# Expert weight preparation in halves over nine attention turns, and bulk transfers behind a slot's transposes, in an attention and two-layer mixture-of-experts kernel

## The chip, the cores and the metric

The kernel runs on one core of a Trainium2 chip. The metric is the device time of one execution in microseconds, the median of several runs; lower is better.

## What is computed

Attention with pooled keys, then two mixture-of-experts layers that send each token to one of eight experts:

```python
kv_pool = kv.reshape(B, H // r, r, W // r, r, C).mean(axis=(2, 4))
k = v = kv_pool.reshape(B, -1, C) @ w_sr
s = scale * (q @ k.transpose(0, 2, 1))
a = np.exp(s - s.max(-1, keepdims=True))
a /= a.sum(-1, keepdims=True) + 1e-09
x = (a @ v).reshape(B * S, D)
...
expert_idx = np.argmax(logits, axis=1)
for e in range(E):
    mask = expert_idx == e
    h = np.maximum(x[mask] @ w1[e], 0.0)
    out[mask] = gate_w[mask, None] * (h @ w2[e])
```

B is 2, there are 24,576 queries in all, 768 keys a batch, C and D are 128, E is 8 and the hidden size F is 1024. The first layer takes its logits from `x @ w_gate`, the second from the normalized rows and expert embeddings over `tau`.

## The kernel before

**Attention** works on 48 groups of 512 tokens. `plan` is a list of steps, each with a lag in turns: in turn n the step `K3:3` is done for group n - 3, tile 3. A turn therefore holds steps of seven groups, and every engine takes its instructions in this written order (`ordered` ties them). Per tile of 128 tokens: scores on TensorE (`at_K`, L531), negated row maxima on VectorE (`at_N`, L538), exponentials on ScalarE (`at_E`, L545), then two 16-bit parts whose sum is the probability, the high part on ScalarE (`at_S`, L552) or VectorE (`at_D`), the low part on VectorE (`at_Z`, L561). SP issues a DMA that transposes both parts (`at_t`, L568) into one of three buffers `aT`; the products with the values read them (`at_A`, L575 to L577), ScalarE copies the sum to `xT` (L582), TensorE multiplies by the first layer's gate (`at_R`, L603), and the routing (`route`) ends with four indirect DMAs of GpSimd that put the rows to their experts' places in DRAM (L491). While the first batch runs, the second batch's `kv` is loaded in pieces of 512 KB (L187).

**Weight preparation.** Matmuls in 16 bits need each weight as a high and a low part at a scale of the expert. For one expert this is: load of `w1` and `w2` into `wraw` (`pw_load`, L340 and L341), sum of squares of both (`pw_square`, L350, ScalarE), scales (`pw_dve`), high parts on ScalarE (L358), low parts on VectorE (L374), and the store of `whl` and the scales to DRAM (`pw_store`, L383 and L385). `wraw` and `whl` have one buffer each. It has five phases. In attention, phase p of expert i stands in turn 2 + 9i + 2p: the steps `ul`, `ua`, `ug` and `uw` of `plan` stand for load, ScalarE, VectorE, and store and first square. So five of the first layer's eight experts are ready when attention ends. The other three, and then the scales of the second layer's eight (whose parts are made in the slots), are prepared beside the slots of the first layer by the steps `vl`, `va`, `vg`, `vs` of `plan_1`, five turns an expert, later three.

**Slots.** Both layers work on slots: 512 rows of one expert (`slot_new`). A slot's turn has eight slices; `both` has the steps of both layers, `plan_1` those of the first. `W0` and `W1` load its two weights into one of two buffers if the expert has changed (`slot_w`, L868), `X` loads its rows transposed (`slot_load`, L930), `H` and `Y` are the two products in eight chunks each (L955 to L957, L974 to L976), `h` and `g` the two parts of the ReLU on ScalarE (L960) and VectorE (L965), and `p` and `n` take steps of `slot_post`. In the first layer `slot_post` issues two DMA transposes of the result (L1000), GpSimd adds their two parts (L1012), ScalarE squares them (L1017), and routing for the second layer follows. `H0` is in slice 2 two turns after the slot's number, `Y0` in slice 6 of that turn, the transposes are in slice 7 of the next.

A list of slots is made by `table`, which runs a few small VectorE instructions at each `.` of a plan; there are eight in a slot's turn. At its end it writes 512 rows of zeros behind each expert's rows (L799), 260 KB each.

The first slots begin before attention has ended. The rest of the attention turns is emitted between the slot's steps:

```python
            while pos < (n0 + i + m / len(plan_l) + DN) * len(plan):
                pos = next(rest_, 1 << 30)
```

Here i is the slot's turn and `pos` the place in the attention's steps; `DN` is 0.

Of the kernel before, what the change touches and what calls it, by code (L numbers as in the profile page):

```python
# [8 lines left out]
F32 = mybir.dt.float32  # L9
# [11 lines left out]
P = 128  # L21
C = 128
# [49 lines left out]
def _body(ctx, tc, q, kv, w_sr, w_gate, w1a, w2a, emb, tau, w1b, w2b, out):  # L72
# [261 lines left out]

    def pw_load(i, ph):

        if ph == 0:
            l, e = divmod(i, E)
            raw = p1.tile([P, 2, F], F32, tag="wraw", name=f"wraw{i}")
            SP.dma_start(raw[:, 0, :], (w1a, w1b)[l][e])  # L340
            SP.dma_start(raw[:, 1, :].rearrange("p (f d) -> p f d", d=C),  # L341
                         (w2a, w2b)[l][e].rearrange("(f p) d -> p f d", p=P))
            pw[i] = [raw, None, None, None]

# [6 lines left out]

    def pw_act(i, ph):
        raw, ss, sc, hl = pw[i]
        if ph == 1:
            pw_square(i, 1)
        elif ph in (3, 4) and i < E:
            k = ph - 3
            A.activation(hl[:, 2 * F * k:2 * F * k + F], raw[:, k, :], AF.Copy, scale=sc[:, k:k + 1])  # L358
# [18 lines left out]
    def pw_store(i, ph):  # L377
        if ph == 0:
            pw_square(i, 0)
        if ph == NPH - 1:  # L380
            l, e = divmod(i, E)
            _, _, sc, hl = pw.pop(i)
            ins = [SP.dma_start(WS[l][e * P:(e + 1) * P, :], sc).ins]  # L383
            if l == 0:
                ins.append(SP.dma_start(WT[e * P:(e + 1) * P, :], hl).ins)  # L385
                if e >= EA:
                    for w in ins:
                        for r in w_reads:
                            tc.declare_no_dep(w, r, reason="weights of other experts")
                    w_late.extend(ins)  # L390
# [244 lines left out]
    U0 = 2  # L635
    UW = 2 if NA1 else 1
    UP = 2 * NPH - 1 if NA1 else NPH

    def at_u(g, fn):

        i, ph = divmod(g - U0, UP)
        if 0 <= i < EA and ph % UW == 0 and ph // UW < NPH:
            fn(i, ph // UW)


    def table(info, l, kind, ns, nh=0, prev=None, left=None):
# [149 lines left out]
        if kind != "a":  # L796
            for e in range(E):
                r = sp_val(bi[0:1, e:e + 1], NROW - TG)
                ins = SP.dma_start(XS[l].rows[bass.ds(r, TG), :].rearrange("(p r) c -> p r c", r=4), zrows)  # L799
                XS[l].wrote(ins.ins)  # L800
                if e % 2:
                    yield
            info["upto"] = XS[l].mark()
# [334 lines left out]
    for n, ((i, w0, m), t) in enumerate(zip(parts, tl)):  # L1138
# [13 lines left out]
        if n == 6:  # L1152
# [8 lines left out]
             "Z": at_Z, "t": at_t, "A": at_A, "x": at_x, "r": at_r, "R": at_R, "w": at_w, "l": at_l, "o": at_o, "p": at_p,  # L1161
             "ul": lambda g: at_u(g, pw_load), "ua": lambda g: at_u(g, pw_act),
             "ug": lambda g: at_u(g, pw_dve), "uw": lambda g: at_u(g, pw_store)}
    plan = """
# [53 lines left out]
    def pw_all(steps_):  # L1218
        for i in steps_:
            for fn in (pw_load, pw_act, pw_dve, pw_store):  # L1220
                fn(*divmod(i, NPH))
# [48 lines left out]
    def run(*a):  # L1270
        for _ in turns(*a):
# [4 lines left out]
              "g": slot_hL, "Y": slot_y, "B": slot_raw, "C": slot_hi, "D": slot_lo}  # L1276
    wsteps = {"vl": pw_load, "va": pw_act, "vg": pw_dve, "vs": pw_store}

# [3 lines left out]
    plan_1 = """  # L1282
        - - p:5 p:4 n:5 - p:4 p:4 / W0:1 n:4 p:5 p:4 n:5 - p:5 p:4 p:5 p:4 / X:1 vl:0 p:5 n:5 - p:5 n:4 vg:1 n:4 p:4 /
        - n:4 p:5 n:4 - p:4 p:4 p:4 / - n:4 p:5 - p:4 - vs:1 / p:3 W1:1 n:4 p:5 - - n:4 /
        - p:3 p:3 n:4 p:3 - n:4 va:0 n:4 / - n:4 p:3 - n:4 p:4 - n:4"""
    plan_2 = """
# [29 lines left out]
    last_a = NG + max(lags)  # L1316
    DN = 0

# [93 lines left out]
```

## Time and profile before

| | |
|---|---|
| median of 3 runs | 1737.48 us (1734.93 to 1743.86) |
| profiled execution | 1748.93 us, of which the span of instructions is 1747.2 us |
| mean granted TensorE clock | 0.975 |
| TensorE busy | 1594.9 us, 91% |
| VectorE busy | 1441.0 us, 82% |
| ScalarE busy | 1328.0 us, 76% |
| moved by DMA | 240.61 MB, 138 GB/s on average |

The busy share is an average over attention (up to about 640 us), the first layer (to about 1220 us) and the second. A turn of attention is counted here from one write of `xT` to the next (ScalarE, L582, one for each group), a slot from its first matmul (L955) to that of the next slot. In a view of windows the columns of an engine give its busy time in the window and, in brackets, its instructions; then come the granted clock, the mean busy share of the DMA engines (packets overlap, so that it can pass 1) and the bytes moved per time. In a timeline a bracket at the end of a row gives how long the engine sat idle before it and what ended that.

### The profile page before, as it was taken

How to read it: one execution, taken by the hardware profiler on the slowest of the kernel's cores; microseconds unless marked ns; L12 is line 12 of the kernel's file. 1: busy time of each engine (PE TensorE's matmuls, PEld its weight loads, DVE VectorE, ACT ScalarE, POOL GpSimd, SP SyncE). 2: the span in 40 equal slices, each digit the busy share in tenths (PEclk: the TensorE clock that was granted, in tenths of full speed). 3: DMA queues.
4: the chain of work that ended last, by engine and by line, in shares of the span. 5: the costliest groups of instructions: out<-in, count | busy, mean ns of one | idle time of the engine just before them, and what ended most of it. 6: DMA issues, size and time to landing. Idle time of an engine off the chain costs nothing.

```text
span 1747.2 us, 31671 instructions
## 1 busy us (share of the span) xinstructions
PE 1594.9 (91%) x8713; PEld 890.4 (51%) x8713; DVE 1441.0 (82%) x3887; ACT 1328.0 (76%) x2731; POOL 982.0 (56%) x1298
## 2 busy tenths in 40 slices
PE   6888988989888789899999999998999999999996
PEld 6666656656666534444444444444444444444443
DVE  5898989989899757787788787787998888888875
ACT  3777778878777746776777877776888888888885
POOL 1386665665565646565666666665544444444453
PEclk9899999999999999999999999999999999999998
DMA  7999998999999953444665455445337335343353
GB/s 247 218 236 201 173 225 174 207 209 179 218 181 190 189 108 78 110 109 113 145 160 123 98 112 106 74 95 128 76 77 175 78 76 127 75 83 74 77 121 63
DMA packets 631019, 240.61 MB, mean 138 GB/s; under 512 B 578464, under 2 KB 604202, under 8 KB 629168
## 3 DMA queue, kind: packets, MB, share of 16 engines
q1 hardware_dynamic: 611776, 200.31, 57.5%
q0 software_dynamic: 18752, 38.18, 8.2%
q8 instruction: 70, 1.15, 0.3%
q14 instruction: 117, 0.96, 0.2%
q10 hardware_dynamic: 304, 0.01, 0.0%
HBM read 148.53 MB, written 52.02 MB: 115 GB/s over the span
## 4 chain that ended last, share of the span: by engine, by line
PE 57%; DVE 18%; issue 8%; DMA 7%; ACT 6%; POOL 3%; SPq 0%; POOLq 0%; ACTq 0%; DVEq 0%
PE ps L957 7%; PE ps L955 7%; PE ps L974 7%; PE ps L956 7%; PE ps L976 7%; PE ps L975 7%; PE ps L531 5%; DVE hL L965 4%; DMA aT<-ab 3%; DVE ab L561 3%; DMA rowss<-yHLs 2%; DVE nm L538 2%; PE ps L575 2%; ACT ab L552 2%; PE ps L577 2%
## 5 line engine op out<-in xcount | busy, mean ns | idle before, releaser
L965 DVE SCALAR_TENSOR_TENSOR hL<-ps,hH 128x512 f16<-128x512 f32 (+1 forms) x808 | 540.0, 672 | 168.6 <-ACT hH L960 114.6
L960 ACT ACTIVATE hH<-ps 128x512 f16<-128x512 f32 (+1 forms) x808 | 466.7, 584 | 174.4 <-PE ps L957 144.2
L1075 POOL DMA_INDIRECT out_dram<-rowss,idxs x198 | 211.4, 1068 | 258.9 <-DVE idxs L1072 157.7
L974 PE MATMUL ps<-hH,wbuf 128*128 128x512 f16 (+1 forms) x808 | 304.1, 376 | 7.3 <-ACT hH L960 7.1
L491 POOL DMA_INDIRECT xs<-rowsa,idxa x192 | 202.6, 1055 | 189.5 <-DVE sca L431 143.1
L976 PE MATMUL ps<-hL,wbuf 128*128 128x512 f16 (+1 forms) x808 | 303.9, 376 | 1.3
L975 PE MATMUL ps<-hH,wbuf 128*128 128x512 f16 (+1 forms) x808 | 304.0, 376 | 0.0
L957 PE MATMUL ps<-x,wbuf 128*128 128x512 f16 (+1 forms) x808 | 304.0, 376 | 0.0
L955 PE MATMUL ps<-x,wbuf 128*128 128x512 f16 (+1 forms) x808 | 304.0, 376 | 0.0
L956 PE MATMUL ps<-x,wbuf 128*128 128x512 f16 (+1 forms) x808 | 303.8, 376 | 0.0
L491 POOL DMA_INDIRECT xs<-rowss,idxs x196 | 204.9, 1046 | 61.6 <-issue 26.8
L545 ACT ACTIVATE a<-ps,nm 128x768 f32<-128x768 f32 x192 | 171.9, 896 | 64.2 <-DVE nm L538 63.1
L561 DVE SCALAR_TENSOR_TENSOR ab<-a,ab 128x768 f16<-128x768 f32 x192 | 201.1, 1047 | 9.9 <-ACT ab L552 9.9
L538 DVE TENSOR_REDUCE nm<-ps 128x1 f32<-128x768 f32 x192 | 181.4, 945 | 32.6 <-PE ps L531 17.9
L552 ACT ACTIVATE ab<-a 128x768 f16<-128x768 f32 x192 | 161.1, 839 | 32.2 <-DMA aT<-ab 28.0
L918 DVE SCALAR_TENSOR_TENSOR wbuf<-wbuf,wsl 128x512 f16<-128x512 f32 x204 | 151.9, 745 | 0.0
L575 PE MATMUL ps<-aT,v 128*128 128x512 f16 x288 | 112.9, 392 | 42.8 <-DMA aT<-ab 33.2
L910 ACT ACTIVATE wbuf<-wbuf,wsl 128x512 f16<-128x512 f32 x204 | 146.0, 716 | 4.7 <-DMA wbuf<-in_moe_w_dram 4.6
L531 PE MATMUL ps<-kH,qH 128*128 128x384 f32 x384 | 129.4, 419 | 9.9 <-ACT a L545 8.8
L975 PEld LDWEIGHTS <-wbuf 128*128 128x128 f16 x808 | 79.4, 98 | 94.5 <-issue 11.3
L976 PEld LDWEIGHTS <-wbuf 128*128 128x128 f16 x808 | 79.4, 98 | 92.6 <-issue 2.2
L957 PEld LDWEIGHTS <-wbuf 128*128 128x128 f16 x808 | 79.4, 98 | 92.5 <-issue 2.2
(391 smaller groups left out, 2892.9 us busy)
## 6 DMA issues: line engine op xcount, KB each, us to landing
wbuf<-in_moe_w_dram SPq DMA_DIRECT2D x102, 512.0 KB
wbuf<-wt SPq DMA_DIRECT2D x98, 512.0 KB
wraw<-in_moe_w_dram SPq DMA_DIRECT2D x32, 512.0 KB
q<-in_q_dram SPq DMA_DIRECT2D x48, 256.0 KB
wt<-whl SPq DMA_DIRECT2D x8, 1024.0 KB
kv<-in_kv_dram SPq DMA_DIRECT2D x12, 512.0 KB
xs<-zrows SPq DMA_DIRECT2D x18, 260.0 KB
out_dram<-rowss,idxs POOLq DMA_INDIRECT x198
```

Of the source, the lines that this page charges most:

```text
L491: ins = G.indirect_dma_start(out=XS[l].rows, out_offset=bass.IndirectOffsetOnAxis(ap=idx[:, r:r + 1], axis=0), in_=rows[:, r, 0:RW], in_of ...
L531: PE.matmul(sv[:, h, :], lhsT=d[x][:, P * t:P * (t + 1)], rhs=k[:, 384 * h:384 * (h + 1)], start=k is kH and x == "qH", stop=x == "qL")
L538: V.tensor_reduce(d["nm"][:, t:t + 1], scores(g, t), axis=AX.XY, op=ALU.max, negate=True)
L561: V.scalar_tensor_tensor(ab[:, 1, :], st[g].pop(("a", t)), AS, ab[:, 0, :], op0=ALU.mult, op1=ALU.subtract)
L955: PE.matmul(hb, lhsT=wL, rhs=s.xH, start=True, stop=False)
L956: PE.matmul(hb, lhsT=wH, rhs=s.xH, start=False, stop=False)
L957: PE.matmul(hb, lhsT=wH, rhs=s.xL, start=False, stop=True)
L960: A.activation(hH, ps[:, f % 4, 0:s.W], AF.Relu)
L965: V.scalar_tensor_tensor(hL, ps[:, f % 4, 0:s.W], 0.0, s.h[f][0], op0=ALU.max, op1=ALU.subtract)
L974: PE.matmul(s.acc, lhsT=wL, rhs=hH, start=f == 0, stop=False)
L975: PE.matmul(s.acc, lhsT=wH, rhs=hH, start=False, stop=False)
L976: PE.matmul(s.acc, lhsT=wH, rhs=hL, start=False, stop=f == NF - 1)
```

## The change

- The five experts of attention: load of `w1` in turn 0 of nine and of `w2` in turn 1, the first square in turn 2, the second and the sum over partitions in turn 3, scales in turn 4, the first weight's parts in turn 5 and its store in turn 6, the second's in turns 7 and 8. `pw_store` is split: its store is now `pw_out`.
- In the first layer's slots, `vl` (load), the new `vt` (store) and `W1` (second weight of a slot) move to slice 8, behind the transposes of slice 7.
- `table` pauses twice after each block of zeros; before, once after each second block.
- `DN` is 1: attention's last turns run one turn earlier against the slots.

```diff
-    def pw_load(i, ph):
+    def pw_load(i, ph, parts=(0, 1)):
         if ph == 0:
             l, e = divmod(i, E)
-            raw = p1.tile([P, 2, F], F32, tag="wraw", name=f"wraw{i}")
-            SP.dma_start(raw[:, 0, :], (w1a, w1b)[l][e])
-            SP.dma_start(raw[:, 1, :].rearrange("p (f d) -> p f d", d=C),
-                         (w2a, w2b)[l][e].rearrange("(f p) d -> p f d", p=P))
-            pw[i] = [raw, None, None, None]
+            if 0 in parts:
+                raw = p1.tile([P, 2, F], F32, tag="wraw", name=f"wraw{i}")
+                pw[i] = [raw, None, None, None]
+                SP.dma_start(raw[:, 0, :], (w1a, w1b)[l][e])
+            if 1 in parts:
+                SP.dma_start(pw[i][0][:, 1, :].rearrange("p (f d) -> p f d", d=C),
+                             (w2a, w2b)[l][e].rearrange("(f p) d -> p f d", p=P))
...
+    def pw_out(i, ph, parts=(0, 1)):
         if ph == NPH - 1:
             l, e = divmod(i, E)
-            _, _, sc, hl = pw.pop(i)
-            ins = [SP.dma_start(WS[l][e * P:(e + 1) * P, :], sc).ins]
+            _, _, sc, hl = pw[i]
+            ins = []
+            if 1 in parts:
+                pw.pop(i)
+                ins.append(SP.dma_start(WS[l][e * P:(e + 1) * P, :], sc).ins)
             if l == 0:
-                ins.append(SP.dma_start(WT[e * P:(e + 1) * P, :], hl).ins)
+                c0, c1 = 2 * F * parts[0], 2 * F * (parts[-1] + 1)
+                ins.append(SP.dma_start(WT[e * P:(e + 1) * P, c0:c1], hl[:, c0:c1]).ins)
...
+    turns_u = {("l", 0): lambda i: pw_load(i, 0, (0,)), ("l", 1): lambda i: pw_load(i, 0, (1,)),
+               ("w", 2): lambda i: pw_store(i, 0), ("a", 3): lambda i: pw_act(i, 1), ("g", 3): lambda i: pw_dve(i, 1),
+               ("g", 4): lambda i: pw_dve(i, 2), ("a", 5): lambda i: pw_act(i, 3), ("g", 5): lambda i: pw_dve(i, 3),
+               ("w", 6): lambda i: pw_out(i, NPH - 1, (0,)), ("a", 7): lambda i: pw_act(i, 4),
+               ("g", 7): lambda i: pw_dve(i, 4), ("w", 8): lambda i: pw_out(i, NPH - 1, (1,))}
...
-                if e % 2:
-                    yield
+                yield
+                yield
...
     plan_1 = """
-        - - p:5 p:4 n:5 - p:4 p:4 / W0:1 n:4 p:5 p:4 n:5 - p:5 p:4 p:5 p:4 / X:1 vl:0 p:5 n:5 - p:5 n:4 vg:1 n:4 p:4 /
-        - n:4 p:5 n:4 - p:4 p:4 p:4 / - n:4 p:5 - p:4 - vs:1 / p:3 W1:1 n:4 p:5 - - n:4 /
-        - p:3 p:3 n:4 p:3 - n:4 va:0 n:4 / - n:4 p:3 - n:4 p:4 - n:4"""
+        - - p:5 p:4 n:5 - p:4 p:4 / W0:1 n:4 p:5 p:4 n:5 - p:5 p:4 p:5 p:4 / X:1 p:5 n:5 - p:5 n:4 vg:1 n:4 p:4 /
+        - n:4 p:5 n:4 - p:4 p:4 p:4 / - n:4 p:5 - p:4 - vs:1 / p:3 n:4 p:5 - - n:4 /
+        - p:3 p:3 n:4 p:3 - n:4 va:0 n:4 / - n:4 p:3 vt:1 vl:0 W1:1 n:4 p:4 - n:4"""
...
-    DN = 0
+    DN = 1.0
```

**Order on SP in attention.** The second of four such places: the store of expert 1's parts (`whl1`), and the load of expert 2 (`wraw2`); `aT` are the transposes of probabilities. Before:

```order
L568 DMA_TRANSPOSE aT15_2506<-ab15_3_2540 128x12x128
L383 DMA ws0_141<-wsc1_2033 128x4
L385 DMA wt_140<-whl1_1502 128x4096
L568 DMA_TRANSPOSE aT16_2653<-ab16_1_2604 128x12x128
L503 DMA q20_2746<-in_q_dram 128x512
L340 DMA wraw2_2754<-in_moe_w1_dram 128x1024
L341 DMA wraw2_2754<-in_moe_w2_dram 128x8x128
L568 DMA_TRANSPOSE aT16_2653<-ab16_2_2661 128x12x128
```

and now (the other half of the store stands eleven rows ahead of the first of these):

```order
L392 DMA ws0_141<-wsc1_2034 128x4
L395 DMA wt_140<-whl1_1799 128x2048
L578 DMA_TRANSPOSE aT16_2655<-ab16_1_2608 128x12x128
L513 DMA q20_2748<-in_q_dram 128x512
L342 DMA wraw2_2756<-in_moe_w1_dram 128x1024
L578 DMA_TRANSPOSE aT16_2655<-ab16_2_2663 128x12x128
L578 DMA_TRANSPOSE aT17_2805<-ab17_0_2669 128x12x128
L578 DMA_TRANSPOSE aT16_2655<-ab16_3_2690 128x12x128
L578 DMA_TRANSPOSE aT17_2805<-ab17_1_2758 128x12x128
L513 DMA q21_2896<-in_q_dram 128x512
L344 DMA wraw2_2756<-in_moe_w2_dram 128x8x128
```

The store has half its columns here, and four transposes stand between the two loads.

**Order on SP in layer 0**, the turn in which expert 6 (`whl6`) is stored and expert 7 (`wraw7`) is loaded; `rowss` are the transposes of a slot's result, `wbuf` and `wsl` a slot's second weight and scales. Before:

```order
L930 DMA_TRANSPOSE x0_14_9700<-xs0_138 128x2x512
L932 ISA
L932 DMA gt0_14_9701<-xs0_138 128x4x4
L340 DMA wraw7_9710<-in_moe_w1_dram 128x1024
L341 DMA wraw7_9710<-in_moe_w2_dram 128x8x128
L383 DMA ws0_141<-wsc6_9304 128x4
L385 DMA wt_140<-whl6_8943 128x4096
L868 ISA
L868 DMA wbuf1_7213<-wt_140 128x2048
L868 ISA
L868 DMA wsl1_7214<-ws0_141 128x4
L1000 DMA_TRANSPOSE rowss0_12_9812<-yHLs0_12_9787 128x4x128 x2
```

and now:

```order
L955 DMA gt0_14_9706<-xs0_138 128x4x4
L1023 DMA_TRANSPOSE rowss0_12_9810<-yHLs0_12_9787 128x4x128 x2
L392 DMA ws0_141<-wsc6_9309 128x4
L395 DMA wt_140<-whl6_8948 128x4096
L342 DMA wraw7_9853<-in_moe_w1_dram 128x1024
L344 DMA wraw7_9853<-in_moe_w2_dram 128x8x128
L891 ISA
L891 DMA wbuf1_7311<-wt_140 128x2048
L891 ISA
L891 DMA wsl1_7312<-ws0_141 128x4
```

The transposes went ahead of all bulk transfers of the turn, and the store ahead of the load.

**Order on TensorE where attention ends**: the gate's matmuls (`iwg`), slot 0 (`x_1`, `wbuf`) and the products of group 46 (`aT` with the values `v`). Before:

```order
L577 MATMUL ps<-aT_6960,v_268 128x512
L603 MATMUL ps<-iwg,xT_7224 128x136 x2
L955 LDWEIGHTS wbuf_6246
L955 MATMUL ps<-x_1_7081,wbuf_6246 128x512
L956 LDWEIGHTS wbuf_6246
L956 MATMUL ps<-x_1_7081,wbuf_6246 128x512
```

and now:

```order
L587 MATMUL ps<-aT_6965,v_268 128x512
L613 MATMUL ps<-iwg,xT_7216 128x136 x4
L585 LDWEIGHTS v_269
L585 MATMUL ps<-aT_7102,v_269 128x512
L586 LDWEIGHTS v_268
```

Slot 0's first twelve matmuls, which stood ahead of group 46's products, stand behind them, and the products of the last group, 47, stand between slot 0's matmuls instead of behind them.

## Rows read from the trace of the kernel before

**Rows 1.** The page's first part: busy time, share and instructions of each engine.

```profile
PE 1594.9 (91%) x8713; PEld 890.4 (51%) x8713; DVE 1441.0 (82%) x3887; ACT 1328.0 (76%) x2731; POOL 982.0 (56%) x1298
```

**Rows 2.** Windows of attention: seven plain turns, four with kv, a long one, four long ones.

```profile
core 0: us, PE busy (x) PEld busy (x) DVE busy (x) ACT busy (x) POOL busy (x), PEclk, DMA share, GB/s
274.60:352.70 78.10, 70.47 (x419) 50.61 (x419) 76.23 (x187) 63.98 (x125) 49.94 (x63) 1.00 1.01 198
...
74.30:123.70 49.40, 44.24 (x274) 33.33 (x272) 48.09 (x113) 38.52 (x75) 40.91 (x46) 1.00 1.10 234
...
246.60:263.10 16.50, 12.25 (x64) 9.03 (x64) 11.30 (x28) 9.94 (x21) 8.44 (x11) 0.79 1.03 221
...
sum 67.00, PE 47.73 PEld 34.54 DVE 44.91 ACT 39.85 POOL 36.23; mean PE 11.93 PEld 8.64 DVE 11.23 ACT 9.96 POOL 9.06
```

**Rows 3.** Timeline of SP's issues around a long turn (start us, us, instruction).

```profile
236.97 0.34 SPq L385 DMA_DIRECT2D wt<-whl  x1
...
241.86 0.44 SPq L340 DMA_DIRECT2D wraw<-in_moe_w_dram  x1
...
242.88 10.90 SPq L568 DMA_TRANSPOSE aT<-ab  x4
```

**Rows 4.** Timeline of all engines in the same turn: the two waits for transposes.

```profile
251.64 0.84 ACT L552 ACTIVATE ab<-a 128x768 f16<-128x768 f32 x1 [3.32 <-DMA aT<-ab]
...
254.36 0.61 PE L575 MATMUL ps<-aT,v 128*128 128x512 f16 x1 [4.25 <-DMA aT<-ab]
```

**Rows 5.** Windows of the store's and of the load's transfer in that turn.

```profile
239.00:242.20 3.20, 2.34 (x13) 1.55 (x12) 3.17 (x12) 2.93 (x5) 0.30 (x2) 1.00 1.04 330
244.30:248.00 3.70, 3.65 (x26) 2.85 (x26) 3.70 (x10) 3.28 (x6) 3.08 (x4) 1.00 1.06 335
```

**Rows 6.** DMA issues between 74.3 and 123.7 us.

```profile
kv<-in_kv_dram SPq DMA_DIRECT2D x6, 512.0 KB
```

**Rows 7.** Windows of layer 0: three plain slots, one pair, three pairs, zero rows.

```profile
965.30:998.20 32.90, 32.66 (x198) 15.57 (x197) 26.34 (x98) 26.25 (x71) 22.28 (x33) 1.00 0.48 106
...
773.00:802.60 29.60, 25.10 (x132) 11.05 (x131) 21.12 (x93) 17.95 (x49) 16.35 (x21) 0.88 0.57 125
...
sum 82.80, PE 71.42 PEld 31.96 DVE 60.39 ACT 53.84 POOL 47.68; mean PE 23.81 PEld 10.65 DVE 20.13 ACT 17.95 POOL 15.89
...
813.50:837.30 23.80, 22.07 (x132) 10.27 (x131) 18.93 (x72) 17.77 (x47) 13.58 (x20) 1.00 0.54 145
```

**Rows 8.** Timeline of SP's issues in the pair of 773.0 to 802.6 us.

```profile
777.23 0.36 SPq L340 DMA_DIRECT2D wraw<-in_moe_w_dram  x1
...
778.76 0.43 SPq L385 DMA_DIRECT2D wt<-whl  x1
...
780.41 4.49 SPq L1000 DMA_TRANSPOSE rowss<-yHLs  x2
```

**Rows 9.** Timeline of all engines in that pair: the waits behind the transposes.

```profile
790.92 1.15 POOL L1012 TENSOR_TENSOR y32s<-rowss 128x512 f32<-128x512 f16 x1 [7.33 <-DMA rowss<-yHLs]
...
793.62 0.38 PE L974 MATMUL ps<-hH,wbuf 128*128 128x512 f16 x1 [2.63 <-ACT hH L960]
```

**Rows 10.** Timeline of SP's issues: blocks of zeros.

```profile
811.60 5.14 SPq L799 DMA_DIRECT2D xs<-zrows  x6
```

**Rows 11.** Timelines of TensorE and ScalarE where attention ends.

```profile
617.27 0.38 PE L575 MATMUL ps<-aT,v 128*128 128x512 f16 x1 [3.90 <-DMA aT<-ab]
...
643.28 0.18 PE L446 MATMUL ps<-cnta,tri 128*128 128x32 bf16 x1 [2.38 <-DVE cnta L441]
...
624.52 0.60 ACT L960 ACTIVATE hH<-ps 128x512 f16<-128x512 f32 x1 [7.53 <-PE ps L957]
```

**Rows 12.** TensorE's timeline at a pause elsewhere, and the window behind it.

```profile
190.42 1.72 PE L603 MATMUL ps<-iwg,xT 128*128 128x136 f32 x8 [2.32 <-DVE ua L470]
...
190.90:194.30 3.40, 3.40 (x13) 2.83 (x13) 3.40 (x10) 2.23 (x5) 0.58 (x2) 0.50 0.61 118
```

**Rows 13.** Instructions of line 350, the squares (duration ns min/median/max).

```profile
L350 ACT ACTIVATE whl<-wraw x32: 1040/1048/1073, 34.8 to 1094.4; 128x1024 bf16<-128x1024 f32 x32
```

More of the change, by code (lines that the diff above doesn't have):

```diff
@@ L352, in pw_act @@
     def pw_act(i, ph):
+        if ph == 0:
+            return
         raw, ss, sc, hl = pw[i]
@@ L635, in _body, with at_u @@
     U0 = 2
-    UW = 2 if NA1 else 1
     UP = 2 * NPH - 1 if NA1 else NPH
-    def at_u(g, fn):
-        i, ph = divmod(g - U0, UP)
-        if 0 <= i < EA and ph % UW == 0 and ph // UW < NPH:
-            fn(i, ph // UW)
+    turns_u = {("l", 0): lambda i: pw_load(i, 0, (0,)), ("l", 1): lambda i: pw_load(i, 0, (1,)),
[3 more added lines that the diff above has]
+               ("g", 7): lambda i: pw_dve(i, 4), ("w", 8): lambda i: pw_out(i, NPH - 1, (1,))}
+    parts_u = {"l": (pw_load,), "a": (pw_act,), "g": (pw_dve,), "w": (pw_store, pw_out)}
+    def at_u(g, o):
+        i, ph = divmod(g - U0, UP)
+        if not 0 <= i < EA:
+            return
+        if NA1:
+            if (o, ph) in turns_u:
+                turns_u[o, ph](i)
+        else:
+            for fn in parts_u[o]:
+                fn(i, ph)
     def table(info, l, kind, ns, nh=0, prev=None, left=None):
@@ L1161, in _body @@
              "Z": at_Z, "t": at_t, "A": at_A, "x": at_x, "r": at_r, "R": at_R, "w": at_w, "l": at_l, "o": at_o, "p": at_p,
-             "ul": lambda g: at_u(g, pw_load), "ua": lambda g: at_u(g, pw_act),
-             "ug": lambda g: at_u(g, pw_dve), "uw": lambda g: at_u(g, pw_store)}
+             "ul": lambda g: at_u(g, "l"), "ua": lambda g: at_u(g, "a"),
+             "ug": lambda g: at_u(g, "g"), "uw": lambda g: at_u(g, "w")}
     plan = """
@@ L1219, in pw_all @@
         for i in steps_:
-            for fn in (pw_load, pw_act, pw_dve, pw_store):
+            for fn in (pw_load, pw_act, pw_dve, pw_store, pw_out):
                 fn(*divmod(i, NPH))
@@ L1276, in _body @@
               "g": slot_hL, "Y": slot_y, "B": slot_raw, "C": slot_hi, "D": slot_lo}
-    wsteps = {"vl": pw_load, "va": pw_act, "vg": pw_dve, "vs": pw_store}
+    wsteps = {"vl": pw_load, "va": pw_act, "vg": pw_dve, "vs": pw_store, "vt": pw_out}
     both = """
```

## The prediction

> **What bounds the kernel now.** I read the busy shares first, then turn by turn the attention part and slot by slot layer 0, then the issue order on SP around the long turns. No engine is full over the whole span: TensorE has 91%, VectorE 82% [rows 1], so the bound must be found for each stage.
>
> In the attention part a turn (one group of 512 tokens) is bound by VectorE. In seven plain turns from 274.6 to 352.7 us VectorE is busy for 76.23 of 78.10 us; a turn takes 11.16 us and VectorE is idle for 0.27 us in it [rows 2]. Once in nine turns one turn is longer: the four together take 67.00 us, and VectorE works for only 44.91 of these [rows 2]. What happens there is seen on SP: at 236.97 it issues the 1 MB store of one expert's parts, at 241.86 the 1 MB load of the next expert, and the issue of the four transposes behind them takes 10.90 us [rows 3]. In the same turn ScalarE waits 3.32 us for a transpose to release its buffer, and TensorE 4.25 us for transposed probabilities [rows 4]. The store's and the load's stretches move 330 and 335 GB/s [rows 5], so 2.1 MB take 6.4 us of transfer time at one place. The clock falls with it: 0.79 of full in that turn, 1.00 in the plain ones [rows 2].
>
> Layer 0 is bound by TensorE: three plain slots take 32.90 us with TensorE busy for 32.66, so 10.97 us a slot [rows 7]. Three pairs of slots stand out, 82.80 us for six slots [rows 7]. They are the three turns in which the last three experts of this layer are stored and the next loaded: loads at 777.23, store at 778.76, and right behind them the two transposes of the slot's result [rows 8]. These land so late that GpSimd waits 7.33 us for them; ScalarE, which squares GpSimd's sum in its own order, holds up the ReLUs behind that, and TensorE stops for 2.63 us [rows 9]; the clock of the pair is 0.88 [rows 7]. Layer 1 has no such stretch, and the change leaves it alone but for its weights' preparation.
>
> **The change, part by part.** The sum is made against the profiled execution (1748.93 us around a span of 1747.2). It is 11.45 us over the median of the runs, 1737.48; I take the same difference off the median.
>
> *Attention: loads and store in halves over nine turns.* The work stays the same: ten squares, parts and products move to other turns, the square for instance is 1048 ns of ScalarE wherever it stands [rows 13], and ScalarE is not the bound there (63.98 of 78.10 us, rows 2); VectorE's part moves by one turn. I cost these at nothing. What goes is the pile of 2.1 MB. If all four long turns become plain ones, the gain is 67.00 - 4 x 11.16 = 22.4 us. What comes in its place is four turns of nine that carry a transfer of 512 KB each, 1.6 us at 330 GB/s [rows 5], 16 of them in the four piles. Their price has bounds: between 74.3 and 123.7 us the load of the second batch's keys issues six transfers of this very size in four turns [rows 6], and VectorE idles 1.31 of 49.40 us [rows 2]; less 0.27 us a turn this is 0.04 us each. The other end is 1.6 us each, all of it uncovered. I take 0.25, near the first, since it is the same size in the same stage, but above it, since those turns last 12.35 us and leave more room than 11.16. So 4.0 us are given back and the term is 18.4 us. The five extra issues on SP cost nothing by themselves: an issue takes 0.34 us there [rows 3], and SP waits for its data most of the time.
>
> The Trainium skill speaks against this part: "DMA: Bandwidth & Descriptors", section Bandwidth, wants transfers batched to at least 1 MiB, and its section "Anatomy of one DMA" gives each a fixed cost of about 2.0 us. By that, an estimate, five stores cut in two would cost 10 us more, the term would be 8.4 us and the sum 1712.7. The six 512 KB transfers do not show such a cost, and their fixed part lies beside other transfers.
>
> *Layer 0: store, load and the second weight half behind the transposes.* If the six slots become plain, 82.80 - 6 x 10.97 = 17.0 us go. The transposes then have no bulk ahead of them, and the 2.1 MB have until the next turn's transposes, 10.97 us for 6.4 us of transfer. Two things get later. The first square of the loaded expert stands on ScalarE about six eighths of a turn after the issue, 8 us; store and first half of the load need 3.2 + 1.6 us at these rates, behind some 2 us until packets flow (issue at 236.97, rows 3; the stretch begins at 239.0, rows 5), so 6.8 us. It may wait up to 1 us, and behind it stand ReLUs for which TensorE waits. The second weight half has six eighths of a turn, 8.2 us, until the first product that reads it, and follows at most 2.1 MB: little room, but most slots keep their weights and load nothing. I put 1 us on each of three turns for both: term 14.0 us, bounds 17.0 and 0.
>
> *Zero rows.* They are issued nearly together, six within 5.14 us [rows 10], and the two slots there take 23.80 us [rows 7], 1.9 us over two plain ones. Spread over two turns they should cost little; I take 1.4, bounds 1.9 and 0. The slot list is ready 1.5 turns later; in the new order the last of these writes still stands ahead of the transposes of a slot three before the first that uses it.
>
> *Attention's tail one turn earlier against the slots.* TensorE now takes the last-but-one group's products ahead of slot 0's first matmuls, and the last group's inside slot 0. Before, TensorE waits 3.90 us for the transposes, then 2.38 us for routing of the last group, and ScalarE stands 7.53 us at a ReLU in front of attention's work [rows 11]. Both waits can go, 6.3 us; or slot 0 just starts a turn later with nothing to fill the wait, a loss up to 11.16 us. The first wait stays, I think, with less work ahead of it, and the second goes under slot 0's matmuls: I take a gain of 1 us.
>
> Sum: 18.4 + 14.0 + 1.4 + 1.0 = 34.8 us, so 1714.1 for the profiled execution and **1702.7 us** for the median.
>
> **The rivals.** *The transfers are the bound in attention.* For it: the DMA share is 1.01 even in plain turns [rows 2], and four long turns lose 22.4 us, close to 4 x 6.4 us of transfers. Then halves cost as much as wholes, and only the other terms remain: 1737.5 - 16.4 = 1721.1 us. Against it: VectorE's 0.27 us of idle time in plain turns, and the six transfers. The rule on 1 MiB that the Trainium skill gives in "DMA: Bandwidth & Descriptors" would go this way.
>
> *The late weights take the place of the late transposes.* If square or second weight half is over 2 us late, TensorE stops as long as it did at 793.62 [rows 9], with the clock behind it, and layer 0 keeps its 17.0 us: 1737.5 - 20.8 = 1716.7 us. For it: 6.8 of 8 us are used. With both rivals true it is 1735.
>
> *Slower: four pauses in place of one.* Every 512 KB chunk pushes the transposes behind it back by 1.6 us. If plain turns have no room left, TensorE pauses in each of 16 turns. A pause of 2.32 us is followed by 3.40 us at a granted clock of 0.50 [rows 12], which loses 1.7 us. That is 16 x (1.6 + 1.7) = 52.8 us against 38.8 of gain: 1751.5 us. It decides where chunk and ordinary jitter together reach a pause like that of rows 12. Against it stand the six chunks again, at a clock of 1.00 [rows 2].
>
> **How the numbers follow.** Forecast 0.72, transfers as the bound 0.11, late weights 0.10, both 0.04, four pauses 0.03. The forecast's own range is 1690 (all terms at their best: 21.8 + 17.0 + 1.9 + 6.3 = 47 us) to 1713; with the two rivals' times it becomes 1690 to 1724. A measurement of this kernel can tell about 0.5%, 8.7 us, from no change. Faster by more: 0.72 + 0.11 + 0.10 = 0.93; within: 0.04; slower: 0.03.
>
> **What would show it.** Right: no turn over 15 us behind a store and load, VectorE at 97% between 130 and 560 us, GpSimd's total wait for the result's transposes well under before, pairs of slots near 22 us. Wrong: TensorE waits for transposes in many turns of 12 to 13 us (transfers are the bound); ScalarE idle ahead of a square, or TensorE ahead of a second product, in three turns of layer 0 (late weights); many half-clock stretches (four pauses); a wait of over 8 us ahead of slot 0 (the tail).

## The result, and the profile after

The changed kernel takes 1724.79 us (median of 7 runs, 1720.69 to 1730.45). The kernel before takes 1742.53 us in the seven runs beside it, so the ratio is 0.9899, 95% interval [0.9876, 0.9923]: faster by 17.6 us (13 to 22), where 34.8 us were forecast. The sign was right; the time lies 0.8 us above the range given. Its profiled execution took 1720.69 us around a span of 1718.9.

The page's first part, against [rows 1]: the same work in 28 us less. Some 10 us of these 28 are scatter and not gain: the profiled execution of the kernel before (1748.93 us) took longer than any of its seven runs, that of the changed kernel was the shortest of its seven.

```profile
PE 1584.7 (92%) x8713; PEld 888.2 (52%) x8713; DVE 1440.4 (84%) x3887; ACT 1325.9 (77%) x2731; POOL 992.0 (58%) x1298
```

**Attention** hardly moved. The first window below is the whole stage, from the first copy to `xT` to the 45th, in the kernel before, the second the same stretch of the changed kernel. A turn is in this part the time between two copies.

```profile
core 0: us, PE busy (x) PEld busy (x) DVE busy (x) ACT busy (x) POOL busy (x), PEclk, DMA share, GB/s
63.90:596.80 532.90, 463.57 (x2688) 337.45 (x2687) 489.68 (x1208) 409.27 (x789) 327.35 (x404) 0.96 1.01 200
```

```profile
62.70:590.00 527.30, 464.24 (x2688) 339.22 (x2688) 489.01 (x1207) 409.89 (x791) 333.03 (x402) 0.96 1.03 202
```

VectorE's work is the same, 489 us; what it did not work fell from 43.2 to 38.3 us only, and the clock stayed at 0.96. The windows of five successive turns of the changed kernel show where the time is lost. The last row is the stretch behind the pause of the third.

```profile
417.50:429.30 11.80, 10.03 (x61) 7.52 (x62) 11.75 (x28) 10.01 (x19) 9.16 (x12) 1.00 1.12 232
429.30:439.90 10.60, 10.00 (x59) 6.79 (x57) 10.57 (x25) 8.64 (x17) 6.91 (x9) 1.00 0.95 196
439.90:454.30 14.40, 11.62 (x61) 8.31 (x62) 11.33 (x28) 9.13 (x19) 10.37 (x12) 0.88 1.16 206
454.30:465.60 11.30, 9.81 (x62) 7.28 (x61) 10.33 (x26) 8.98 (x18) 6.70 (x9) 1.00 1.14 251
465.60:476.80 11.20, 9.71 (x61) 7.20 (x60) 10.27 (x26) 8.73 (x17) 6.70 (x9) 1.00 1.22 201
446.50:449.90 3.40, 3.40 (x10) 1.95 (x9) 1.29 (x4) 2.67 (x6) 2.65 (x3) 0.54 1.14 264
```

The third takes 14.40 us with VectorE at 11.33. SP's timeline has the bulk issues of these turns:

```profile
442.81 0.43 SPq L395 DMA_DIRECT2D wt<-whl  x1
...
446.38 0.44 SPq L342 DMA_DIRECT2D wraw<-in_moe_w_dram  x1
446.92 11.40 SPq L578 DMA_TRANSPOSE aT<-ab  x4
...
459.33 0.44 SPq L344 DMA_DIRECT2D wraw<-in_moe_w_dram  x1
```

The second half of the store and the first half of the next load stand 3.6 us apart, in one turn; the second half of the load follows one turn later. (An earlier half of the store stands alone, in the first of the five turns, which is not long.) TensorE's timeline has the wait, where [rows 4] had one of 4.25:

```profile
446.36 0.58 PE L585 MATMUL ps<-aT,v 128*128 128x512 f16 x1 [2.29 <-DMA aT<-ab]
```

So a long turn of 16.75 us per expert (67.00 / 4, rows 2) has become, here, one of 14.40 and two of over 11 with VectorE idle for 1 us in each. The pause of the third turn ends at 446.36, before the load's half is issued (446.38), so it stands behind the store's half alone. The other three turns that carry a half of the store and a half of the next load are not long like this one:

```profile
123.60:135.30 11.70, 10.71 (x68) 7.92 (x66) 11.67 (x26) 8.99 (x18) 10.57 (x12) 1.00 1.06 268
229.60:242.10 12.50, 10.03 (x61) 7.52 (x62) 11.86 (x31) 8.97 (x17) 8.60 (x12) 1.00 1.14 245
337.70:347.30 9.60, 9.60 (x61) 7.09 (x60) 9.28 (x26) 8.71 (x18) 5.29 (x7) 1.00 1.07 254
```

The four pauses of 4 to 5 us of before have become more and shorter ones, behind single halves as well: between 123 and 561 us TensorE's products wait for transposes 16 times, 23.5 us in all and at most 3.2 at once, before 13 times, 22.1 us and at most 5.0.

**Layer 0** did move. The windows of the three pairs of slots that [rows 7] gives 82.80 us, and then three slots between two pairs, in the changed kernel:

```profile
695.70:720.40 24.70, 22.23 (x132) 10.39 (x131) 20.34 (x82) 17.78 (x49) 15.43 (x21) 1.00 0.68 151
755.50:779.50 24.00, 22.23 (x132) 10.38 (x131) 19.80 (x83) 17.65 (x49) 15.43 (x21) 1.00 0.69 155
813.60:837.50 23.90, 22.03 (x132) 10.31 (x131) 18.13 (x63) 18.10 (x49) 15.42 (x21) 1.00 0.63 155
720.40:755.50 35.10, 33.08 (x199) 15.69 (x198) 32.10 (x134) 25.98 (x69) 22.34 (x30) 1.00 0.34 70
```

The pairs take 72.6 us. GpSimd's wait for the transposes of the result, 7.33 us in [rows 9], is now:

```profile
707.61 1.15 POOL L1035 TENSOR_TENSOR y32s<-rowss 128x512 f32<-128x512 f16 x1 [1.44 <-DMA rowss<-yHLs]
```

The longest such wait between 695 and 838 us is 2.3 us. But ScalarE now waits ahead of the first square in all three pairs, which it did nowhere before; the first of these waits:

```profile
713.87 1.06 ACT L352 ACTIVATE whl<-wraw 128x1024 bf16<-128x1024 f32 x1 [1.87 <-DMA wraw<-in_moe_w_dram]
```

**The tail.** TensorE still stands for 3.68 us ahead of the last products, as forecast (3.90 us in rows 11); but where rows 11 names the transposes, "issue" in this row means that the profile shows nothing that was waited for. The wait for the last group's routing went from 2.38 to 1.13 us:

```profile
606.09 0.38 PE L585 MATMUL ps<-aT,v 128*128 128x512 f16 x1 [3.68 <-issue]
...
633.09 0.18 PE L456 MATMUL ps<-cnta,tri 128*128 128x32 bf16 x1 [1.13 <-DVE cnta L451]
```

### The profile page after: what moved, and what is told of

Same layout as the page of the kernel before. It is cut to its first block, busy times and chain, and to the rows that moved or that the text cites. A ratio compares the mean times of both kernels' runs of the same rounds, so it can differ in the third digit from the quotient of the medians.

```text
span 1718.9 us, 31617 instructions
## 1 busy us (share of the span) xinstructions
PE 1584.7 (92%) x8713; PEld 888.2 (52%) x8713; DVE 1440.4 (84%) x3887; ACT 1325.9 (77%) x2731; POOL 992.0 (58%) x1298
## 3 DMA queue, kind: packets, MB, share of 16 engines
q8 instruction: 70, 1.15, 0.3%
## 4 chain that ended last, share of the span: by engine, by line
PE 36%; issue 21%; DVE 17%; POOL 10%; DMA 8%; ACT 6%; SPq 1%; POOLq 0%; DVEq 0%; ACTq 0%
POOL out_dram L1098 6%; PE ps L541 5%; DMA aT<-ab 5%; PE ps L997 4%; PE ps L999 4%; PE ps L978 4%; PE ps L998 4%; PE ps L980 4%; PE ps L979 4%; DVE hL L988 4%; DVE ab L571 3%; DVE nm L548 2%; PE ps L585 2%; PE ps L586 2%; PE ps L587 2%
## 5 line engine op out<-in xcount | busy, mean ns | idle before, releaser
L562 ACT ACTIVATE ab<-a 128x768 f16<-128x768 f32 x192 | 161.0, 839 | 25.3 <-DMA aT<-ab 23.8
```

## The experiments

The runs of one group below were made on one chip beside the kernel before, whose median there lay between 1741.58 and 1748.37 us from chip to chip; so ratios to it are compared.

### The four parts alone (p1 to p4)

Each is the kernel before with one part of the change: the turn table of the halves (p1_att), `plan_1` (p2_slots), the two `yield` of the zero rows (p3_zero), `DN = 1.0` (p4_tail).

> The kernel before with the attention part alone: loads, squares, parts and stores of the five experts in halves over nine turns. As predicted, the four long turns become plain ones: 18 us faster (0.990). If the transfers bind, the same bytes cost the same: no change (0.999 to 1.001), with VectorE's idle time between 64 and 596 us at some 43 us as before. The trace of the whole change, where attention's turns 0 to 44 were only 5.6 us shorter, says 3 to 8 us faster (0.995 to 0.998), with pauses of 1.3 to 2.6 us behind single halves and some half-clock stretches.

> The kernel before with the first layer's part alone: load, store and second weight of a slot behind the slot's transposes. As predicted 14 us faster (0.992), the three pairs near 23 us each. If late weights take the place of late transposes: no change (0.998 to 1.002), with TensorE waiting for a weight's transfer or ScalarE ahead of a square.

> The kernel before with the blocks of zeros spread alone. As predicted 1.4 us faster (0.999), which the timing can hardly show; the two slots at the first list's zeros, 23.8 us before, should take 22.0 to 22.5 us. The rival, that the blocks were hidden anyway or now stand ahead of other transposes, gives no change there.

> The kernel before with attention's tail one turn earlier against the slots, alone. As predicted 1 us faster, with bounds of 6 us faster and 11 us slower; the trace of the whole change has the stretch from the last-but-two write of xT to the third slot's first matmul 3.4 us shorter. If slot 0 merely starts a turn later, it is 5 to 11 us slower.

| | ratio [95%] | us at 1744.4 | forecast |
|---|---|---|---|
| p1_att | 0.9977 [0.9963, 0.9992] | -4.0 | -18.4 |
| p2_slots | 0.9956 [0.9940, 0.9971] | -7.7 | -14.0 |
| p3_zero | 1.0007 [0.9994, 1.0020] | +1.2 | -1.4 |
| p4_tail | 0.9962 [0.9945, 0.9979] | -6.6 | -1.0 |

The sum, -17.1, with an interval of some 5 us to either side, is the whole's -17.6: that the parts disturb one another does not show, and attention's term is what failed most. The two slots at the zeros, for which 22.0 to 22.5 us were expected, take 23.2 in p3_zero:

```profile
811.90:835.10 23.20, 21.93 (x131) 10.21 (x130) 19.93 (x70) 17.91 (x47) 14.90 (x20) 1.00 0.56 156
```

p3_zero has the old order in layer 0, and its windows of the three pairs are a second sample of [rows 7]:

```profile
710.10:737.60 27.50, 23.89 (x132) 10.70 (x131) 20.11 (x84) 17.90 (x49) 15.12 (x20) 0.94 0.61 135
773.20:800.50 27.30, 22.39 (x131) 10.26 (x130) 19.49 (x86) 17.72 (x49) 14.99 (x20) 1.00 0.61 136
835.10:861.20 26.10, 22.52 (x132) 10.29 (x131) 18.60 (x63) 17.94 (x49) 15.00 (x20) 1.00 0.59 143
```

They are 80.9 us, the middle one at a clock of 1.00 and not 0.88 and 27.3 us and not 29.6.

### What a half costs: bytes, place or distance (q1 to q3, q6, q5)

Theory A is the rival of the prediction, no room in the queues; B, the place inside the turn; C, halves that add up because they come in the same or in successive turns. All edits are on the changed kernel. q4_dn2 went along.

```diff
# q1_more
+               ("l", 3): lambda i: pw_more(i),
+    def pw_more(i):
+        l, e = divmod(i, E)
+        SP.dma_start(pw[i][3].bitcast(F32)[:, F:2 * F], (w1a, w1b)[l][e])
# q2_place: ux issues the store halves; the square stays in uw
-        q:0 K3:3 ul:0 S1:3 p:6
+        q:0 K3:3 S1:3 p:6
...
-        S2:3 t3:4 E0:2
+        S2:3 t3:4 ul:0 ux:0 E0:2
# q3_space
-    turns_u = {("l", 0): lambda i: pw_load(i, 0, (0,)), ("l", 1): lambda i: pw_load(i, 0, (1,)),
-               ("w", 2): lambda i: pw_store(i, 0), ("a", 3): lambda i: pw_act(i, 1), ("g", 3): lambda i: pw_dve(i, 1),
-               ("g", 4): lambda i: pw_dve(i, 2), ("a", 5): lambda i: pw_act(i, 3), ("g", 5): lambda i: pw_dve(i, 3),
-               ("w", 6): lambda i: pw_out(i, NPH - 1, (0,)), ("a", 7): lambda i: pw_act(i, 4),
-               ("g", 7): lambda i: pw_dve(i, 4), ("w", 8): lambda i: pw_out(i, NPH - 1, (1,))}
+    turns_u = {("l", 1): lambda i: pw_load(i, 0, (0,)), ("l", 3): lambda i: pw_load(i, 0, (1,)),
+               ("w", 2): lambda i: pw_store(i, 0), ("a", 4): lambda i: pw_act(i, 1), ("g", 4): lambda i: pw_dve(i, 1),
+               ("g", 5): lambda i: pw_dve(i, 2), ("a", 6): lambda i: pw_act(i, 3), ("g", 6): lambda i: pw_dve(i, 3),
+               ("w", 6): lambda i: pw_out(i, NPH - 1, (0,)), ("a", 8): lambda i: pw_act(i, 4),
+               ("g", 8): lambda i: pw_dve(i, 4), ("w", 8): lambda i: pw_out(i, NPH - 1, (1,))}
# q4_dn2
-    DN = 1.0
+    DN = 2.0
```

> The changed kernel, with the first weight matrix of each of the five experts of the attention stage loaded a second time, into a part of the parts' tile that is still free: 512 KB more per expert, issued at the start of a turn that has no bulk transfer, two turns from the nearest one that has. Theory A (the DMA engines have no room in attention, so every 512 KB keeps the transposes late by about its own transfer time, and a half costs 1.0 to 1.5 us wherever it stands): 5 to 8 us slower than the changed kernel, ratio to the kernel before 0.993 to 0.995 against 0.990. Theory B (the halves are late for the transposes behind them because they are issued ahead of them in the turn): as A. Theory C (a half alone in its turn is hidden, only the halves of successive turns add up): within 1 us of the changed kernel, ratio 0.990.

> The changed kernel, with the issue of every half, loads and stores, moved inside its turn to right behind the transpose that completes the tile's four (t3), so that the transpose that the weighted sums wait for is ahead of the bulk transfer and the next such one a whole turn away. Theory A (no room): within 3 us of the changed kernel, ratio 0.988 to 0.992. Theory B (place in the turn): 6 to 15 us faster than the changed kernel, ratio 0.981 to 0.987; the pauses at the weighted sums of 2 us and more are gone. Theory C (successive turns): within 2 us.

> The changed kernel, with the two load halves in the second and fourth of the nine turns in place of the first and second, and the squares, scales and parts moved to fit, so that the four halves of an expert lie 2, 2, 2 and 3 turns apart in place of 2, 1, 1 and 5. Theory A (no room): within 3 us of the changed kernel, ratio 0.988 to 0.992. Theory B (place in the turn): as A. Theory C (successive turns add up): 5 to 12 us faster, ratio 0.983 to 0.987, and the pauses behind the second load half are gone.

> The changed kernel, with the last attention steps two turns ahead of the slots' steps (DN = 2.0 in place of 1.0). If the gain of 6.6 us of the first turn is TensorE's order at the end of attention, with its waits for the last transposes filled: another 1 to 4 us faster, ratio 0.988 to 0.989. If one turn is enough and the second only delays the first slots: 0 to 5 us slower, ratio 0.990 to 0.993.

Measured: q1_more 0.9904 [0.9876, 0.9932], q2_place 0.9855 [0.9826, 0.9884], q3_space 0.9835 [0.9808, 0.9863], q4_dn2 0.9899 [0.9877, 0.9922]. Against 0.9899 the extra half cost 1 us, the distance gave 11 us, as C said, and the place 8, as B said. Each of these differences has an interval of some 6 us to either side, so q1_more alone does not exclude A. A second turn of `DN` gives nothing.

Next came the changed kernel itself (r0_after), only the loads one turn later (q6_later), spacing and place together (q5_both), and the rival of the late second weight (q7_w1).

```diff
# q6_later
-    turns_u = {("l", 0): lambda i: pw_load(i, 0, (0,)), ("l", 1): lambda i: pw_load(i, 0, (1,)),
+    turns_u = {("l", 1): lambda i: pw_load(i, 0, (0,)), ("l", 2): lambda i: pw_load(i, 0, (1,)),
# q5_both: q3_space, and in plan
-        q:0 K3:3 ul:0 S1:3 p:6
+        q:0 K3:3 S1:3 p:6
...
-        S2:3 t3:4 E0:2
+        S2:3 t3:4 ul:0 E0:2
# q7_w1
-        p:3 vt:1 vl:0 W1:1 n:4
+        p:3 W1:1 vt:1 vl:0 n:4
```

> The changed kernel itself, for a ratio on the same chip as the three beside it. Both theories: ratio to the kernel before 0.988 to 0.992.

> The changed kernel, with both load halves one turn later (second and third of the nine turns), squares and the rest where they are: the store half and the load half that fell in one turn are apart, the two load halves still come in successive turns. Theory C1 (what adds up is the store half and the load half 4 us apart): gets most of what the spacing of all four gave, 6 to 11 us faster than the changed kernel in the same call. Theory C2 (the two load halves in successive turns add up): within 3 us of the changed kernel, since they follow one another as before. Theory A (no room, the cost goes by bytes): within 2 us.

> The spacing of q3 (second and fourth turns) together with the loads' place behind the completing transpose, stores where they are. If spacing and place are two parts of one lateness (a half needs a stretch of its own before the next transpose that is waited for): 0 to 4 us faster than the spacing alone, ratio 0.980 to 0.984. If place has a gain of its own: 6 to 10 us faster than the spacing alone, ratio 0.977 to 0.980.

> The changed kernel, with the second weight matrix of the next expert (W1) issued ahead of the store and the load in its slice of the first layer's slots, in place of behind them. If the late second weight is what layer 0 still loses (five waits at the second layer's matmuls for wbuf, 9.6 us in all): 4 to 9 us faster than the changed kernel in the same call. If those waits are covered by VectorE or the weight only moves ahead of the slots' transposes: within 2 us.

Measured: r0_after 0.9909 [0.9884, 0.9933], q6_later 0.9866 [0.9835, 0.9897], q5_both 0.9823 [0.9795, 0.9851], q7_w1 0.9896 [0.9864, 0.9929]. Taking the load half out of the store half's turn alone gives 7.5 us (C1, with an interval of 7 us to either side), although the two load halves still come in successive turns. How it gives them the traces don't show: in q6_later's profiled execution the turn with the store's second half is as long as in the changed kernel, with nearly the same pause, though no load stands in it. Shorter is the turn behind it, 9.60 us against 11.30:

```profile
440.40:454.60 14.20, 11.61 (x61) 8.54 (x62) 11.23 (x28) 9.14 (x18) 9.71 (x12) 0.88 1.20 221
454.60:464.20 9.60, 9.60 (x61) 7.09 (x60) 9.29 (x26) 8.72 (x17) 5.30 (x7) 1.00 0.94 214
```

```profile
446.69 0.38 PE L585 MATMUL ps<-aT,v 128*128 128x512 f16 x1 [2.13 <-DMA aT<-ab]
```

q5_both is 2 us below q3_space in the ratio: place adds little to spacing, as the first of its two expectations said. It took 1708.06 us, 16.7 less than the changed kernel beside it (1724.75), and is the version to take from this study. Its attention stage:

```profile
61.40:575.50 514.10, 454.90 (x2687) 334.04 (x2686) 485.88 (x1206) 411.13 (x791) 335.28 (x402) 0.98 1.07 208
```

That is 18.8 us below the 532.90 of before; VectorE idles 28.2 us in place of 43.2. q7_w1 shortens the waits it was aimed at. The second product's waits for the weight in the changed kernel, and then in q7_w1 (us, times; a stop that both the weight load and the matmul show counts twice, so that the five are three stops):

```profile
  DMA wbuf<-wt: 9.6, 5
```

```profile
  DMA wbuf<-wt: 3.0, 2
```

The waits ahead of the squares go too (5.6 to 0.6 us), and the three pairs take 70.6 us in place of 72.6. But the whole moves by 2 us with an interval of 7 us to either side: the 4 to 9 us expected are not shown, and 2 us can't be told from none.

### Is the cut needed? (s_ref, s_whole, s_more, t_apart, t_halves; s_dn0)

s_ref is q5_both again; s_whole issues its loads and stores whole, s_more adds a fifth half, s_dn0 is the changed kernel with `DN = 0`.

```diff
# s_whole, against s_ref
-    turns_u = {("l", 1): lambda i: pw_load(i, 0, (0,)), ("l", 3): lambda i: pw_load(i, 0, (1,)),
-               ("w", 2): lambda i: pw_store(i, 0),
+    turns_u = {("l", 2): lambda i: pw_load(i, 0),
+               ("w", 3): lambda i: pw_store(i, 0),
...
-               ("w", 6): lambda i: pw_out(i, NPH - 1, (0,)),
...
-               ("w", 8): lambda i: pw_out(i, NPH - 1, (1,))}
+               ("w", 8): lambda i: pw_out(i, NPH - 1)}
# s_more, against s_ref; pw_more as in q1_more
+               ("l", 5): lambda i: pw_more(i),
```

> The version with spacing and place (q5) once more, as the measure on the same chip for the two beside it. All theories: ratio to the kernel before 0.979 to 0.985.

> As s_ref, but each expert's load is issued whole (1 MB, in the third of the nine turns, behind the completing transpose) and its store whole (in the ninth), so load and store are still 2 and 6 turns apart. If distance alone was what the halves lacked: within 3 us of s_ref. If a turn hides 512 KB and not 1 MB: two pauses of 1.5 to 3 us per expert come back, 8 to 20 us slower than s_ref, ratio 0.987 to 0.994.

> As s_ref, with a fifth half per expert: the first weight matrix is loaded a second time in the sixth of the nine turns, behind the completing transpose, into a part of the parts' tile that is still free. Theory A (no room, the cost goes by bytes, 1.0 to 1.5 us a half): 5 to 8 us slower than s_ref. Theory C (a half with a distance of its own is hidden, 0.25 us or less): 0 to 2 us slower.

> The changed kernel with DN = 0, the last attention steps where they were before among the slots' steps. If the tail is worth in the whole what it gave alone: ratio 0.993 to 0.996, and the stretch from the last full attention turn to the third slot 3 to 5 us longer than in the changed kernel. If the tail is worth the 1 us of the forecast and the rest of 6.6 was the layout of that one program: ratio 0.990 to 0.992.

Measured: s_ref 0.9844 [0.9817, 0.9872], s_whole 0.9859 [0.9830, 0.9888], s_more 0.9821 [0.9794, 0.9848], s_dn0 0.9917 [0.9890, 0.9944]. Five more halves at a distance of their own cost nothing (C); A's 5 to 8 us are refuted. A single profile would have misled here: in the profiled execution of s_more the stage is 10 us longer than in that of s_ref (the first window is s_ref's, the second s_more's), yet s_more's five times lie within 1715.97 to 1719.51 and s_ref's six within 1712.91 to 1725.99.

```profile
62.50:576.40 513.90, 453.28 (x2687) 331.39 (x2686) 482.80 (x1208) 410.56 (x791) 328.86 (x402) 0.99 1.07 208
```

```profile
64.20:588.40 524.20, 456.16 (x2687) 331.86 (x2686) 481.66 (x1208) 410.86 (x791) 333.24 (x404) 0.98 1.09 210
```

Whole transfers came out level with halves, which an account by the bytes of one turn does not give. So the last two runs tried distance without and with the cut on the kernel before, loads at their old place at the turn's start. t_halves has q3_space's table in the kernel before:

```diff
# t_apart, against the kernel before (its turns written as a table)
-    turns_u = {("l", 0): lambda i: pw_load(i, 0), ("w", 0): lambda i: pw_store(i, 0),
-               ("a", 2): lambda i: pw_act(i, 1), ("g", 2): lambda i: pw_dve(i, 1), ("g", 4): lambda i: pw_dve(i, 2),
+    turns_u = {("l", 2): lambda i: pw_load(i, 0), ("w", 3): lambda i: pw_store(i, 0),
+               ("a", 4): lambda i: pw_act(i, 1), ("g", 4): lambda i: pw_dve(i, 1), ("g", 5): lambda i: pw_dve(i, 2),
```

> The kernel before with one thing changed in attention: each expert's load, whole (1 MB) and at its old place in the turn, comes in the third of the nine turns, two turns behind the whole store of the expert before it, in place of the first; squares, scales and parts follow one turn later than before where they must. Nothing is cut. If the long turns of before came from store and load in one place (2.1 MB): 10 to 18 us faster than before, ratio 0.990 to 0.994, where the changed kernel's halves gave 4. If 1 MB in a turn is still too much: 0 to 6 us faster, ratio 0.9965 to 1.000.

> The kernel before with q3's table alone in attention: halves, the loads in the second and fourth turns, places in the turn as in the changed kernel. If distance does it and the cut adds nothing: within 3 us of t_apart. If the cut is needed: 5 to 12 us faster than t_apart, ratio 0.988 to 0.992.

Measured: t_apart 0.9993 [0.9975, 1.0010], t_halves 0.9911 [0.9889, 0.9933]. Distance alone gives nothing, distance with the cut 15.5 us (12 to 19). A whole load was two transfers of 512 KB all along, issued one right behind the other; only the store is cut in two by the change, and the load's two are moved apart. The windows of four turns of t_apart show one pile turned into two: the whole store is issued in the first of them, the whole load in the third, and the turn behind each is long.

```profile
335.27 0.40 SPq L395 DMA_DIRECT2D wt<-whl  x1
...
363.31 0.44 SPq L342 DMA_DIRECT2D wraw<-in_moe_w_dram  x1
363.80 0.42 SPq L344 DMA_DIRECT2D wraw<-in_moe_w_dram  x1
```

```profile
332.60:343.70 11.10, 10.02 (x59) 6.79 (x57) 11.07 (x27) 8.69 (x18) 7.39 (x9) 1.00 1.04 252
343.70:359.60 15.90, 11.64 (x61) 8.56 (x62) 10.81 (x27) 8.97 (x18) 9.16 (x12) 0.89 1.19 187
359.60:369.20 9.60, 9.60 (x61) 7.09 (x60) 9.29 (x26) 8.73 (x17) 5.29 (x7) 1.00 0.87 210
369.20:383.70 14.50, 11.38 (x61) 8.31 (x61) 10.58 (x26) 9.01 (x17) 9.07 (x11) 0.88 1.15 221
```

TensorE's timeline in the second and in the fourth:

```profile
351.65 0.39 PE L585 MATMUL ps<-aT,v 128*128 128x512 f16 x1 [4.25 <-DMA aT<-ab]
...
375.80 0.38 PE L585 MATMUL ps<-aT,v 128*128 128x512 f16 x1 [3.12 <-DMA aT<-ab]
```

The same expert's turns in t_halves, with a half of the store in the first, a half of the load in the second and in the fourth:

```profile
334.20:344.40 10.20, 9.79 (x59) 6.82 (x57) 10.16 (x26) 8.69 (x17) 6.09 (x8) 1.00 0.97 222
344.40:356.60 12.20, 10.03 (x61) 7.53 (x62) 11.10 (x28) 9.00 (x17) 9.25 (x12) 1.00 1.18 224
356.60:366.70 10.10, 9.78 (x61) 7.25 (x60) 9.76 (x26) 8.73 (x17) 5.58 (x8) 1.00 1.10 207
366.70:380.20 13.50, 11.33 (x61) 8.28 (x60) 10.55 (x26) 9.93 (x19) 8.85 (x11) 0.87 1.13 217
```

They take 46.0 us against 51.1. A half with a distance of its own is not always free: in the fourth of these turns TensorE still pauses, and the turn's granted clock is 0.87.

```profile
372.30 0.38 PE L585 MATMUL ps<-aT,v 128*128 128x512 f16 x1 [2.17 <-DMA aT<-ab]
```

One step stays argued and not shown: s_whole differs from t_apart in the load's place behind the completing transpose (and in the slots' parts), so a whole load seems to need that place, and a half does not.

## Why the prediction was wrong

**Attention, forecast 18.4 us, measured 4.0 (1 to 6).** That the four long turns come from store and load, and that most of 18 us can be had there, was right: t_halves gets 15.5. It does not take the whole pile of 2.1 MB, though: in t_apart 1 MB makes turns of 15.90 and 14.50. The step that failed is "What comes in its place is four turns of nine that carry a transfer of 512 KB each ... I take 0.25". It priced a half by its size alone, 4.0 us for 16 of them. In this order a half costs, by an estimate from the times, (22.4 - 4.0) / 16 = 1.15 us; two turns apart it costs (22.4 - 15.5) / 16 = 0.43. The runs that only move issues show that order and place set this price: p1_att and t_halves differ in the turn table alone. The prediction did not look where in the turns the issues stand. The store stands late in its turn and the load at the start of the next, so between two copies to `xT` a turn carries both, 1 MB, and the next one a half more. And the six transfers that gave the price [rows 2, 6] stand elsewhere in their turn, right behind the three transposes of which the last completes a group's four, where q2_place gained 8 us:

```profile
80.57 5.83 SPq L568 DMA_TRANSPOSE aT<-ab  x3
86.46 1.43 SPq L187 DMA_DIRECT2D kv<-in_kv_dram  x1
```

Their turns also last 12.35 us, so place and room are not told apart there. By which waits two neighbouring halves cost more than two separate ones stays open: the traces show pauses behind single halves too.

The rival "The transfers are the bound in attention" has nearly the measured total (1721.1 us), but for the wrong reason: it holds that halves cost as much as wholes, and s_more, t_halves and t_apart refute that. The rival of four pauses fell with the sign, though its mechanism is there in small: pauses of 1 to 3 us, behind some of them a stretch of half clock (0.54 at 446.50 us). The Trainium skill's rule to batch transfers to at least 1 MiB ("DMA: Bandwidth & Descriptors", Bandwidth) would have kept the store whole. It is a rule for throughput. Here t_apart, with the store whole, gave nothing (0.9993) and t_halves 15.5 us, while s_whole came out level with its halves (0.9859 and 0.9844), so the time does not follow the size of a transfer alone. The fixed cost of about 2.0 us that the prediction takes from the Trainium skill ("DMA: Bandwidth & Descriptors", Anatomy of one DMA) is given there for transfers issued by GpSimd, and these are issued by SP. The 10 us that it would make of five more transfers did not show when SP issued five more loads of 512 KB, each alone in its turn (s_more, 0.9821 against 0.9844).

**Layer 0, forecast 14.0, measured 7.7 (5 to 10).** The mechanism was right: the transposes have nothing ahead of them, GpSimd's wait fell to 1.44 us, the clock stays at 1.00. The term was mis-sized twice. "If the six slots become plain, 82.80 - 6 x 10.97" took its plain slots from 965 us on; in this stretch slots with no bulk at all take 11.7 us (35.10 / 3), with VectorE busy for 32.10 of 35.10 us, where the plain ones of rows 7 had 26.34 of 32.90. And 82.80 holds clock losses of one execution; p3_zero has 80.9. From 80.9 to the 72.6 of after is 8.3 us. With both put right the term would have been 80.9 - 6 x 11.7 - 3.0 = 7.7 us, so the 3 us put on late squares and weights were not what was off. The late square did show: ScalarE waits 1.87, 1.94 (in two) and 1.83 us in the three pairs, more than the "up to 1 us" of the prediction. The late second weight shows elsewhere: its three stops, near 866, 900 and 1174 us, lie outside the pairs.

**Zero rows, forecast 1.4, measured -1.2 (-3.5 to 1.0).** The 1.9 us of these two slots over plain ones was the same wrong yardstick: with 11.7 us a slot there are 0.4 us to get, and the slots went from 23.8 to 23.2.

**Tail, forecast 1.0, measured alone 6.6 (4 to 10).** It came out at the upper one of its bounds (-11.16 to 6.3); the first wait stayed, as forecast; the second shrank. But undone in the changed kernel (s_dn0 against r0_after and the first comparison, on other chips) it is worth only 1 to 3 us, with an interval of some 6 us to either side. Its size stays open between these; the 1 us of the forecast was a choice between two bounds, and the runs don't decide it.

**The base.** The sum was taken off 1737.48, a median of three; seven runs give 1742.53. That is 5 us of the 22.1 by which the time was missed.

## What to carry to other kernels

When a pile of transfers is cut up, lay the pieces out against the waits they hold up, not against the numbers of a plan, and try their distance and their place as well as their size. With the loads at the start of a turn, cutting with pieces in successive turns gave 4 us and distance without the cut nothing; both together gave 15.5. With the load behind the transpose that is waited for, whole transfers did as well as halves. Five more transfers of 512 KB, each with a turn of its own, cost nothing. Take the yardstick for "plain" from neighbours in the same stage, and a stage's length from more than one execution.

## What was not expected

The same program's attention stage is not the same from one execution to the next. The changed kernel's window above is 527.30 us, and r0_after, the same program, has the following, where VectorE's work is the same to 0.6 us:

```profile
61.70:593.20 531.50, 462.23 (x2687) 340.16 (x2688) 489.63 (x1207) 410.39 (x791) 332.25 (x404) 0.97 1.04 201
```

Such 4 us are as large as p1_att's whole gain, so only the repeated times could tell it.
